# One more group's up-projection as seven half-size products, in a kernel whose order is written out by hand

## The chip, the core and the metric

The kernel runs on one core of one Trainium2 chip. The core has a matrix engine (TensorE, PE in the profile), a vector engine (VectorE, DVE), a scalar engine (ScalarE, ACT), GpSimd (POOL) and SyncE (SP), each with an instruction queue of its own, worked off strictly in order. The metric is the device time of one execution in microseconds (us); the time before is the median of 3 runs.

## The reference

Sliding-window attention with a distance bias feeds a two-layer network with a squared ReLU. Cut to what matters:

```python
# q, k, v: (8, 8, 576, 64); w_in: (512, 2048); w_out: (2048, 512), all float32
scores = (q @ k.transpose(0, 1, 3, 2)) / sqrt(64)
rel = pos[:, None] - pos[None, :]
scores = where((rel >= 0) & (rel < 128), scores - slopes * abs(rel), -1e9)
x = softmax(scores) @ v                    # -> 4608 tokens x 512
h = x @ w_in
g = maximum(h, 0) ** 2
out = g @ w_out                            # 4608 x 512, float32
```

## The kernel before

The 4608 tokens are cut into 9 groups of 512 (g = 0 to 8), and attention is cut into 40 blocks of up to 128 query tokens (m = 0 to 39), each of which sees its own keys and those of the block before. All matmuls are in bfloat16 with float32 sums in eight PSUM banks.

The program is a list of named tasks. `Plan.order()` does not choose an order: it reads the string `ORDER`, in which the tasks stand in the sequence in which they are emitted, each with its engine (`:a` ACT, `:d` DVE, `:g` POOL, `:s` SP, nothing for PE) and, where it needs one, the number of the PSUM bank, of the float32 buffer `f` (8 of them) or of the buffer `rt` (4). Each engine works its tasks off in that sequence; between engines semaphores keep the dependencies. An item is written `name:engine:places`.

The names, which all later sections use:

- `lkq<m>`, `lv<m>` load keys with queries, and values, from DRAM (POOL's queue, into rings of 4 and 9 tiles); `kqT<m>` turns a block of keys and queries with a DMA transpose (SP's queue, line 675, ring of 7).
- `s<m>.0/.1` are the scores of a block (PE, line 744: matmuls of 64 rows, two at a time on the two halves of the array, 8 per task or 12 for the blocks made of two 64-token ends: 10, 18, 28, 38); `e<m>.0` to `.3` the exponentials (ACT, line 776), `m<m>` the masks (DVE, line 771), `pv<m>` probabilities by values (PE, line 873; for the four two-end blocks lines 850 and 855), `r<m>`, `n<m>` the normalisation (DVE, lines 887 and 900), and `x<m>` the DMA transpose of the result into `xT` (SP, line 907).
- `u<g>.<half>.<e>` is the plain up-projection (line 1020): per task two blocks of 128 hidden units by 256 tokens, 8 matmuls of 256 columns. `relu...` (ACT, line 987) and `sq...` (ACT line 979 or DVE line 981) follow and write `g`.
- `f<g>.<u>.<p>` is the up-projection as seven half-size products (a scheme of Strassen's kind): hidden units and tokens are both halved, as are the 512 inputs, and for each of four column blocks u there are products p = 1, 2, 6, 5, 7, 3, 4, each of 4 matmuls of 256 columns (line 1115). `s1`, `s2`, `s5` copy partial sums from PSUM into an `f` buffer (line 429 on ACT, line 427 on DVE); `c11`, `c22`, `c12` add them with the ReLU in one DVE instruction (line 1136); product 4 takes the plain ReLU. `us<q>.<i>` are sums and differences of blocks of `w_in`, formed once (line 1061), and `ut<g>.<i>` differences of blocks of the group's `xT` (line 1084).
- `p<g>.<p>.<z>` is the down-projection, in all groups as seven half-size products (line 1270; two tasks of 8 matmuls each per product), with `S1` to `S4` (DVE, line 1416), `ws` (line 1228), copies `s1_<g>` and so on, combinations `c11_<g>` and so on (lines 1340, 1351, 1356), and stores `st<g>.<p>.<row>` (SP).

Groups 0, 1 and 2 have the plain up-projection, groups 3 to 8 that of seven products; the constant `G_UP` says from which group on:

```python
def ups(g):
    if g >= G_UP:
        return [("up", g, u, p) for u in range(4) for p in (1, 2, 6, 5, 7, 3, 4)]
```

One of the `us` steps overwrites a quarter of `w_in` in place, so it waits for the up-projections that read the plain weights:

```python
tops = [x for gg in range(G_UP) for x in g_up[gg]]
```

`ut<g>.0` needs all 512 tokens of the group, and the first two products only the first 256:

```python
xs = [x for m in blocks(g * 512, g * 512 + 512) for x in t_x[m]]
xe = [x for m in blocks(g * 512, g * 512 + 256) for x in t_x[m]]
```

Group 2 holds the attention blocks 8, 9, 10 (with 11) and 12. In the list before, the order on PE is: group 1 up, group 0 down, then group 1 down mixed with group 2 up (`u2.0` when the first half of its tokens is there, `u2.1` later), then group 2 down mixed with group 3 up (`f3`), and so on.

Of the kernel before, what the change touches and what calls it, by code (L numbers as in the profile page):

```python
# [100 lines left out]
squ2.0.3:d pv13.0::4 m13.1:d us1.3:d pv13.1::2 r13.1:d r13.0:d n13.0:d n13.1:d p1.6.1 s2_1:d:6 reluu2.0.2:a:3
reluu2.0.5:a:2 reluu2.0.4:a:0 kqT14:s kqT15:s kqT16:s lv14:g lkq17:g lv15:g lv16:g lkq18:g x10:s x12:s s14.0::4,6
s14.1::5,3 s15.0::2,1 p1.3.0 p1.7.0 p1.3.1 e14.0:a e14.2:a e14.1:a e15.0:a e14.3:a e15.1:a s15.1::3,2 s16.0::1,6
s16.1::5,4 e16.0:a e16.2:a e15.3:a e15.2:a e16.1:a p1.7.1 m14.1:d squ2.0.6:d c12_1:d m14.0:d u2.0.0::7 pv14.0::2
pv14.1::5 u2.0.1::3 c22_1:d m15.0:d reluu2.0.0:a:1 e16.3:a m15.1:d r14.0:d squ2.0.2:a r14.1:d n14.0:d pv15.0::6
r15.0:d n14.1:d pv15.1::7 m16.1:d reluu2.0.1:a:3 m16.0:d squ2.0.0:a u2.1.4::2 u2.1.7::5 pv16.0::3 pv16.1::4 kqT17:s
reluu2.1.7:a:1 squ2.0.1:a squ2.0.5:d reluu2.1.4:a:2 squ2.1.7:a r16.0:d n16.0:d r16.1:d r15.1:d n16.1:d n15.0:d
squ2.0.4:d n15.1:d u2.1.5::1 u2.1.6::3 reluu2.1.6:a:1 squ2.1.4:d reluu2.1.5:a:0 squ2.1.6:a u2.1.2::6 u2.1.1::3
reluu2.1.1:a:1 u2.1.0::1 u2.1.3::3 reluu2.1.0:a:2 squ2.1.5:a squ2.1.1:d us2.2:d reluu2.1.2:a:1 squ2.1.2:d squ2.1.0:d
S1.2.0:d s17.1::1,7 s17.0::2,4 p1.4.0 p1.4.1 p2.2.0::6 p2.1.0::5 p2.2.1 e17.0:a reluu2.1.3:a:0 e17.1:a squ2.1.3:a  # L110
m17.0:d us0.2:d S1.2.1:d e17.2:a e17.3:a S2.2.0:d m17.1:d S2.2.1:d lkq20:g lv20:g lkq21:g lv17:g s3_1:a:7 pv17.0::0
r17.0:d us3.2:d n17.0:d st0.3.0:s st0.7.2:s kqT18:s st1.2.0:s st0.2.1:s st0.7.3:s st1.2.1:s st0.2.0:s st1.7.2:s x13:s
x14:s kqT20:s x16:s x15:s s18.0::7,1 s18.1::4,3 pv17.1::2 p2.1.1 p2.5.0::0 p2.5.1 S4.2.0:d S4.2.1:d S3.2.0:d S3.2.1:d
r17.1:d e18.0:a e18.2:a s1_2:a:0 e18.1:a e18.3:a n17.1:d p2.6.0 p2.6.1 lv18:g c11_2:d m18.1:d m18.0:d f3.1.2::6
f3.0.1::2 f3.0.2::3 pv18::1,4 s1.3.0:a:3 s2_2:a:1 us1.2:d ut3.0:d ut3.1:d r18.0:d c11.3.0:d:0 ut3.2:d n18.0:d ut3.3:d
r18.1:d n18.1:d st1.7.3:s st0.3.1:s st1.3.0:s st0.4.3:s kqT21:s f3.0.5::7 f3.0.6 s2.3.0:a:3 p2.7.0 sqc11.3.0:a
s5.3.0:a:2 f3.0.7 f3.1.1::1 f3.1.5::4 f3.0.3 s1.3.1:a:4 c22.3.0:d:0 sqc22.3.0:a c12.3.0:d:2 c11.3.1:d:0 f3.1.6 f3.0.4
reluf3.0.4:a:1 s2.3.1:a:4 p2.7.1 s5.3.1:a:3 sqc12.3.0:d s5_2:d:2 c22_2:d lkq22:g lv21:g lkq23:g lkq24:g lv22:g lv23:g
kqT22:s lkq25:g s20.1::2,6 s20.0::7,3 f3.1.7 c22.3.1:d:2 f3.1.3 e20.0:a e20.2:a e20.1:a e20.3:a c12.3.1:d:3 m20.0:d
f3.2.1::7 p2.3.0 f3.1.4 m20.1:d pv21.0::6 pv20.0::4 f3.2.2::3 pv21.1::2 r20.0:d r21.0:d n21.0:d r21.1:d n21.1:d  # L120
sqc22.3.1:a sqc12.3.1:a reluf3.1.4:a:2 s1.3.2:a:4 sqc11.3.1:a sqf3.0.4:a sqf3.1.4:a p2.4.0 pv20.1::1 p2.3.1 n20.0:d
r20.1:d c11.3.2:d:3 s22.0::4,2 s22.1::3,6 e22.0:a e22.2:a e22.1:a e22.3:a p2.4.1 f3.2.6 f3.3.1::3 f3.2.5::2 s2.3.2:a:4
n20.1:d S1.3.0:d c12_2:d sqc11.3.2:d m22.0:d S2.3.0:d s1.3.3:a:3 x17:s st0.4.2:s st1.3.1:s st2.2.0:s kqT23:s x18:s
s23.1::6,0 s23.0::4,1 e23.0:a e23.1:a e23.3:a e23.2:a f3.2.7 s5.3.2:d:6 kqT24:s x21:s x20:s kqT25:s m22.1:d
c22.3.2:d:3 f3.3.6 f3.2.3 c12.3.2:d:2 sqc12.3.2:d f3.3.2::4 f3.3.5::1 f3.2.4 pv22.0::2 s2.3.3:a:6 s5.3.3:a:4 f3.3.7
# [5 lines left out]
lkq28:g st2.2.1:s st1.4.2:s st2.3.1:s st2.3.0:s st1.4.3:s kqT27:s kqT26:s p3.6.0 p3.6.1 ut4.2:d S3.3.0:d m24.0:d
c11_3:d S3.3.1:d ut4.3:d f4.0.7 c22.4.0:d:0 f4.1.2::4 f4.1.1::3 f4.0.3 p3.5.0::6 s1.4.1:a:5 sqc11.4.0:d f4.0.4 m24.1:d
f4.1.5::0 f4.1.6 c12.4.0:d:3 c11.4.1:d:2 S4.3.0:d m25.0:d m25.1:d pv24.1::4 pv24.0::1 s5.4.1:a:5 p3.5.1 f4.1.3
pv25.1::2 sqc22.4.0:a reluf4.0.4:a:1 r24.0:d r24.1:d n24.0:d n24.1:d pv25.0::1 r25.1:d r25.0:d n25.0:d n25.1:d
sqc12.4.0:d s2_3:a:6 sqc11.4.1:a s2.4.1:a:7 p3.7.0 f4.1.7 c22.4.1:d:2 c12.4.1:d:3 s5_3:d:5 S4.3.1:d s26.0::2,1
s26.1::4,7 e26.0:a e26.3:a e26.2:a e26.1:a p3.7.1 lkq30:g lv26:g lv28:g lv27:g lkq31:g lkq32:g kqT28:s st2.4.2:s x22:s
x23:s kqT30:s x24:s x25:s f4.2.1::2 f4.1.4 f4.2.2::4 reluf4.1.4:a:0 p3.3.0 s27.0::3,1 s27.1::7,0 e27.0:a e27.2:a
e27.3:a c22_3:d sqc22.4.1:d s1.4.2:d:7 c11.4.2:d:2 sqc12.4.1:d sqf4.0.4:d p3.3.1 f4.2.5::4 f4.2.6 s5.4.2:a:7 e27.1:a
p3.4.0 f4.2.3 s28.1::1,0 s28.0::7,3 c12_3:d s2.4.2:a:1 m27.1:d S1.4.0:d m27.0:d m26.0:d S2.4.0:d e28.0:a f4.3.1::6
f4.2.7 s1.4.3:a:0 f4.3.2::7 c11.4.3:d:1 e28.3:a kqT31:s st2.4.3:s st2.7.2:s kqT32:s st3.3.1:s sqc11.4.3:a f4.3.6  # L140
# [1339 lines left out]
```

## Time and profile before

| | |
|---|---|
| median of 3 runs | 289.09 us (289.02 to 289.82) |
| the profiled execution | 289.45 us, of which 286.1 us span from the first to the last instruction |
| granted TensorE clock | 1.00 |
| busy share of the span | PE 97%, weight loads 84%, DVE 85%, ACT 70%, POOL 37% |
| DMA | 39.60 MB, mean 138 GB/s |

The profile is one execution, recorded by the hardware. Busy time is the sum of the times in which an engine had at least one instruction under way. Neighbouring instructions overlap in their first and last stages, so the mean duration of an instruction is longer than the distance to the next one behind it. A row of the chain of waits gives its start, its length and what ran; a row of the timeline the same with the engine and, in brackets, the idle time before it.

### The profile page before, as it was taken

What the parts mean: (1) busy time and instruction counts of PE and PEld (TensorE: products, weight loads), DVE (VectorE), ACT (ScalarE), POOL (GpSimd) and SP (SyncE); (2) the same over time, 40 slices, a digit from 0 to 9 for tenths busy, and PEclk for the clock granted to TensorE, in tenths of its full rate; (3) what the DMA queues carried; (4) which work ended last, traced back from release to release, by engine and by line L of the source; (5) the groups of instructions that cost most, each with busy time, mean ns of one, the idle gap of its engine ahead of it and who ended that gap; (6) DMA issues with size and microseconds to landing.
All of it is one profiled execution on the core that took longest, in us unless ns stands there. A gap on an engine that the chain in (4) does not pass through costs nothing.

```text
span 286.1 us, 8477 instructions
## 1 busy us (share of the span) xinstructions
PE 277.3 (97%) x3403; PEld 240.3 (84%) x3404; DVE 242.2 (85%) x557; ACT 201.3 (70%) x397; POOL 106.3 (37%) x132
## 2 busy tenths in 40 slices
...
GB/s 127 166 196 169 182 200 166 168 154 151 177 151 180 179 155 196 173 141 183 146 163 148 151 173 151 147 187 210 170 93 21 57 93 2 21 95 35 23 112 124
DMA packets 171238, 39.60 MB, mean 138 GB/s; under 512 B 156736, under 2 KB 171200, under 8 KB 171200
## 3 DMA queue, kind: packets, MB, share of 16 engines
...
q8 instruction: 26, 0.43, 0.6%
...
## 4 chain that ended last, share of the span: by engine, by line
PE 93%; DMA 2%; ACT 2%; POOL 1%; DVE 1%; issue 0%; POOLq 0%
PE o L1270 38%; PE h L1115 26%; PE h L1020 14%; PE s L744 6%; PE pv L873 5%; DMA kq<-in_k_dram 2%; POOL kq L609 1%; PE tp L689 1%; ACT P L822 1%; PE xp L920 1%; PE o L1372 1%; ACT rt L987 1%; PE pv L855 1%; ACT masks L474 0%; PE s L813 0%; PE pv L850 0%
## 5 line engine op out<-in xcount | busy, mean ns | idle before, releaser
L1270 PEld LDWEIGHTS <-g 128*128 128x128 bf16 x704 | 67.0, 98 | 8.7
L776 ACT ACTIVATE P<-s 128x512 bf16<-128x512 f32 x120 | 64.0, 609 | 9.9 <-PE s L744 9.7
L1270 PE MATMUL o<-w_out_sb,g 128*128 128x256 bf16 x432 | 53.3, 273 | 0.0
L987 ACT ACTIVATE rt<-h 128x512 bf16<-128x512 f32 (+1 forms) x73 | 42.4, 598 | 14.4 <-PE h L1115 8.5
L1136 DVE CUSTOM_DVE_ANT_0 rt<-h,f 128x512 bf16<-128x512 f32 x72 | 47.8, 682 | 5.0 <-PE h L1115 2.5
L429 ACT ACTIVATE f<-h 128x512 f32<-128x512 f32 x62 | 36.3, 604 | 22.3 <-PE h L1115 18.3
L979 ACT ACTIVATE g<-rt 128x512 bf16<-128x512 bf16 x73 | 45.3, 641 | 3.7 <-DVE rt L1136 3.3
L1020 PE MATMUL h<-xT,w_in_sb 128*128 128x128 bf16 (+1 forms) x512 | 46.3, 246 | 0.1
...
L1020 PEld LDWEIGHTS <-w_in_sb 128*128 128x128 bf16 x512 | 39.0, 98 | 4.1 <-DVE xT L427 0.3
L1115 PEld LDWEIGHTS <-w_in_sb 128*128 128x128 bf16 x384 | 36.5, 98 | 4.5
L1115 PE MATMUL h<-xT,w_in_sb 128*128 128x256 bf16 x288 | 39.1, 273 | 0.0
L771 DVE TENSOR_TENSOR P<-P,masks 128x1024 bf16<-128x1024 bf16 x48 | 32.1, 681 | 4.7 <-ACT P L776 3.9
L1270 PE MATMUL o<-wsum,sums 128*128 128x256 bf16 x288 | 34.9, 273 | 0.0
L1270 PE MATMUL o<-wsum,g 128*128 128x256 bf16 x272 | 34.1, 273 | 0.0
L981 DVE TENSOR_TENSOR g<-rt 128x512 bf16<-128x512 bf16 (+1 forms) x72 | 28.6, 412 | 4.6 <-ACT rt L987 4.2
L1270 PEld LDWEIGHTS <-sums 128*128 128x128 bf16 x288 | 27.6, 98 | 3.5
L1115 PEld LDWEIGHTS <-us 128*128 128x128 bf16 x288 | 27.3, 98 | 3.6
L900 DVE TENSOR_TENSOR x<-pv,rec 128x256 bf16<-128x256 f32 x72 | 28.5, 416 | 0.7
L620 POOL DMA_DIRECT2D vt<-in_v_dram x28 | 24.9, 897 | 9.6 <-DMA kq<-in_k_dram 3.9
L429 ACT ACTIVATE f<-o 128x512 f32<-128x512 f32 x26 | 15.5, 602 | 16.1 <-PE o L1270 15.2
L1115 PE MATMUL h<-ut,us 128*128 128x256 bf16 x192 | 26.5, 273 | 0.0
...
## 6 DMA issues: line engine op xcount, KB each, us to landing
...
w_out_sb<-in_moe_w_out_dram POOLq DMA_DIRECT2D x4, 512.0 KB, 11.8
...
```

Source lines behind the costliest of these rows:

```text
L429: nc.scalar.activation(o, i, AF.Copy)
L620: nc.gpsimd.dma_start(tile_of(s_v[m])[0:n, :, 0:D], source(v, m))
L771: nc.vector.tensor_tensor(flat(Pt[sP.idx], w), flat(Pt[sP.idx], w), flat(mk, w), op=ALU.mult)
L776: nc.scalar.activation(flat(Pt[sP.idx], slice(2 * i, 2 * i + 2)), sS[i].tile.rearrange("p (j t) -> p j t", j=2)[:, :, lo:hi], AF.Exp, bias ...
L900: nc.vector.tensor_tensor(o, heads(sv)[0:n, :, 0:D], sr.tile[0:n, :].unsqueeze(2).to_broadcast([n, 4, D]), op=ALU.mult)
L979: nc.scalar.activation(o, i, AF.Square, bias=0.0, scale=1.0)
L981: nc.vector.tensor_tensor(o, i, i, op=ALU.mult)
L987: nc.scalar.activation(rts[srt.idx][:, 0:n], slot.tile[:, 0:n], AF.Relu, bias=0.0, scale=1.0)
L1020: nc.tensor.matmul(slot.tile[:, f * w:(f + 1) * w], w_in_sb[:, cc, fc * 128:(fc + 1) * 128], xT[:, cc, lo % (XR * 128):lo % (XR * 128) + w ...
L1115: nc.tensor.matmul(slot.tile[:, j * 256:j * 256 + 256], a, b_, start=fresh and j == 0 and c == 0, stop=c == 1, skip_group_check=True)
L1136: nc.vector._custom_dve(TENSOR_ADD_SAT, out=rts[srt.idx], in0=slot.tile, in1=other(), s0=FMAX, s1=0.0)
L1270: nc.tensor.matmul(slot.tile[:, z * 256:z * 256 + 256], stationary(c), moving(c), start=fresh and z == 0 and c == 0, stop=c == F - 1, skip ...
```

## The change

`G_UP` becomes 2, so that group 2 is projected up by seven products as well: the 16 tasks `u2...` with their 16 relus and 16 squares leave, and 28 tasks `f2...`, four `ut2`, twelve copies, twelve combinations, four relus and 16 squares come. The string `ORDER` is new from shortly after its 250th item on: the group-1 down-projection (`p1`) stands ahead of `f2` but for its last task, `f2` stands by itself, and then `p2` begins and runs mixed with `f3`. The `us` steps are done before `f2`. In all later groups tasks, banks and engines are placed anew, with the same tasks as before.

```diff
-G_UP = 3
+G_UP = 2
...
-s1_1:a:3 e10.0:a e10.3:a e10.2:a S1.1.1:d S2.1.0:d S3.1.1:d S2.1.1:d c12_0:d S3.1.0:d S4.1.1:d us2.1:d p0.4.1
-p1.5.0::7 e10.1:a p1.6.0 s12.0::2,6 s12.1::3,1 lkq16:g x9:s p1.5.1 e12.0:a e12.1:a e12.2:a e12.3:a c11_1:d m10.1:d
-m10.0:d us2.3:d pv10::2,5 u2.0.7::6 m12.0:d r10.0:d s5_1:d:4 r10.1:d m12.1:d n10.0:d n10.1:d u2.0.6::1 pv12.0::3
...
+p0.6.1 ws0.3:d s5_0:a:1 s2_0:a:2 S4.0.0:d S1.1.0:d ws1.2:d S1.1.1:d us2.1:d c11_0:d S2.1.0:d S2.1.1:d us2.2:d p0.3.0
+s8.0::2,0 s8.1::6,7 p0.7.0 p0.3.1 p0.7.1 squ1.0.4:a e8.0:a e8.3:a e8.1:a s9.1::0,7 s9.0::4,2 m8.0:d p1.1.0::5 p1.1.1
+c22_0:d S3.1.1:d c12_0:d e9.0:a e9.2:a e8.2:a e9.3:a S3.1.0:d m8.1:d ws1.3:d kqT10:s lv9:g lv10:g lv12:g lkq15:g
+lv15:g lkq13:g lkq14:g lkq16:g lv13:g lv14:g s10.0::1,0 s10.1::6,4 st0.7.2:s kqT13:s kqT15:s e9.1:a m9.1:d e10.0:a
+e10.1:a e10.3:a e10.2:a p1.2.0::7 pv8.1::2 pv8.0::1 p0.4.0 r8.1:d r8.0:d n8.0:d s1_1:d:3 n8.1:d m10.1:d m10.0:d m9.0:d
+p0.4.1 s12.0::6,1 s12.1::2,4 p1.2.1 e12.0:a e12.1:a e12.3:a e12.2:a s3_0:a:4 kqT14:s kqT16:s c11_1:d pv10::6,0 r10.0:d
+pv9.1::1 pv9.0::4 m12.0:d r9.0:d n9.0:d p1.6.0 r9.1:d n9.1:d pv12.0::3 p1.6.1 p1.5.0::1 m12.1:d r10.1:d n10.0:d
+pv12.1::6 r12.0:d n10.1:d s2_1:a:5 s13.0::4,2 s13.1::0,7 p1.7.0 p1.5.1 e13.0:a e13.2:a e13.3:a e13.1:a n12.0:d
+S4.1.1:d us3.2:d us2.3:d r12.1:d n12.1:d m13.1:d S4.1.0:d m13.0:d s15.0::6,7 s14.0::0,4 s14.1::2,3 s5_1:a:6 e15.0:a
+e14.0:a e14.1:a e14.3:a e14.2:a e15.1:a p1.7.1 pv13.1::6 pv13.0::0 p1.3.0 p1.3.1 c22_1:d m14.0:d r13.1:d r13.0:d
+n13.0:d n13.1:d m14.1:d m15.0:d c12_1:d lkq17:g lkq18:g lv16:g x8:s st0.7.3:s x9:s x10:s x12:s st0.3.0:s kqT17:s
+st1.7.2:s st0.3.1:s s16.0::0,7 s15.1::2,3 s16.1::6,4 e16.0:a e16.1:a e16.3:a e15.3:a e15.2:a p1.4.0 m16.0:d pv15.0::0
+pv14.0::7 pv14.1::1 f2.0.1::4 f2.0.2::3 s1.2.0:a:1 ut2.0:d ut2.1:d r14.0:d c11.2.0:d:2 ut2.2:d m15.1:d n14.0:d r14.1:d
+f2.0.5::2 f2.0.6 s5.2.0:a:7 e16.2:a s2.2.0:a:1 p1.4.1 f2.0.3 pv15.1::6 f2.0.7 f2.1.1::7 f2.3.1::3 r15.0:d c12.2.0:d:3
+n14.1:d r15.1:d ut2.3:d c22.2.0:d:1 n15.0:d m16.1:d n15.1:d sqc22.2.0:d s17.0::1,2 s1.2.1:a:1 e17.0:a e17.1:a f2.1.6
+s2.2.1:a:7 f2.0.4 lv18:g lkq20:g lkq21:g lkq22:g lv17:g f2.1.2::1 s17.1::0,2 f2.1.5::6 e17.2:a reluf2.0.4:a:1
+c11.2.1:d:0 sqc11.2.1:d sqc12.2.0:d f2.1.7 s5.2.1:a:1 e17.3:a f2.3.2::1 pv16.0::4 r16.0:d c22.2.1:d:3 n16.0:d
+f2.2.1::0 f2.1.3 f2.2.2::2 f2.1.4 pv16.1::4 c12.2.1:d:0 sqf2.0.4:a s1.2.2:a:1 sqc11.2.0:a c11.2.2:d:1 s1.2.3:a:7
+f2.2.6 f2.2.5::6 r16.1:d n16.1:d c11.2.3:d:2 sqc22.2.1:d f2.3.6 s2.2.2:a:1 f2.2.7 s5.2.2:a:2 f2.3.5::1 f2.2.3
+s2.2.3:a:7 c22.2.2:d:3 sqc11.2.2:d sqc11.2.3:d f2.3.7 sqc12.2.1:a s5.2.3:a:2 c22.2.3:d:1 sqc22.2.2:a m17.1:d m17.0:d
+S1.2.0:d f2.2.4 p2.1.0::4 f2.3.4 reluf2.2.4:a:2 reluf2.1.4:a:3 sqf2.1.4:d sqf2.2.4:a reluf2.3.4:a:0 sqf2.3.4:a f2.3.3
...
```

More of the change, by code (lines that the diff above doesn't have):

```diff
@@ L101 @@
[L101 to L125, printed above, removed]
@@ L131 @@
[L131 to L140, printed above, removed]
@@ new lines @@
+st0.2.1:s st1.2.1:s kqT18:s x14:s x13:s x15:s kqT20:s x16:s kqT21:s kqT22:s s18.1::3,5 s18.0::6,1 e18.0:a e18.2:a
+e18.1:a e18.3:a p2.5.0::2 p2.5.1 p2.6.0 p2.6.1 f3.0.1::5 f3.1.1::1 f3.0.2::3 s1.3.0:a:2 s1.3.1:a:3 S3.2.0:d c11_2:d
+m18.1:d n17.1:d S3.2.1:d ut3.0:d ut3.1:d f3.0.5::7 s5.3.0:a:0 f3.0.6 s2.3.0:a:5 f3.1.6 f3.0.3 f3.1.5::0 c11.3.0:d:0
+m18.0:d ut3.2:d c12.3.0:d:2 ut3.3:d f3.0.7 c22.3.0:d:1 s2.3.1:a:2 s5.3.1:a:6 f3.1.7 s2_2:a:5 f3.1.3 s20.0::7,3
+c22.3.1:d:3 sqc11.3.0:a sqc12.3.0:d c12.3.1:d:0 S4.2.1:d sqc22.3.0:a S4.2.0:d sqc22.3.1:d e20.0:a e20.1:a p2.7.0
@@ new lines @@
+f3.0.4 f3.1.4 reluf3.0.4:a:2 pv18::3,0 s22.0::5,7 reluf3.1.4:a:1 s5_2:a:2 e22.0:a e22.1:a r18.0:d n18.0:d r18.1:d
+n18.1:d p2.7.1 s22.1::3,1 s20.1::5,6 f3.1.2::0 f3.2.1::7 sqc12.3.1:d e20.3:a e20.2:a c22_2:d sqf3.1.4:d m20.0:d lv20:g
+lv21:g lkq23:g lkq24:g lkq25:g lkq26:g lv22:g st1.4.3:s st1.4.2:s kqT23:s kqT24:s st0.4.2:s x17:s kqT25:s st2.2.0:s
+kqT26:s x18:s c11.3.1:d:1 p2.4.0 f3.3.1::5 p2.4.1 m20.1:d e22.3:a s1.3.2:a:6 e22.2:a m22.0:d pv20.0::3 pv21.0::0
+pv20.1::1 pv21.1::6 r20.0:d r21.0:d n20.0:d r20.1:d r21.1:d p2.3.0 n20.1:d n21.0:d n21.1:d f3.2.2::3 c11.3.2:d:0
@@ new lines @@
+s1.3.3:a:3 sqc11.3.1:a f3.2.6 f3.3.6 f3.2.5::6 f3.3.2::3 s2.3.2:a:0 s5.3.2:a:6 s2.3.3:a:7 sqc11.3.2:a x20:s x21:s
+st0.4.3:s st2.2.1:s p2.3.1 S1.3.0:d S2.3.0:d c11.3.3:d:1 sqc11.3.3:a s3_2:a:3 c12_2:d f3.2.7 f3.3.5::0 f3.3.7
+s23.0::2,3 s23.1::4,1 c22.3.2:d:0 m22.1:d sqc22.3.2:d S3.3.0:d f3.2.3 f3.2.4 s5.3.3:a:6 e23.0:a sqf3.0.4:a e23.1:a
+reluf3.2.4:a:2 e23.3:a p3.1.0::2 p3.1.1 c22.3.3:d:0 c12.3.2:d:1 sqf3.2.4:d sqc22.3.3:d e23.2:a m23.1:d f3.3.4 f3.3.3
+c12.3.3:d:0 sqc12.3.3:d reluf3.3.4:a:2 sqf3.3.4:a pv22.0::4 pv22.1::1 r22.0:d n22.0:d r22.1:d s24.0::5,6 s24.1::7,3
@@ new lines @@
+sqc11.4.0:a f4.0.7 f4.1.4 c12.4.0:d:2 c12.4.1:d:3 r23.1:d c22.4.0:d:0 n23.1:d s26.0::5,7 p3.3.0 e26.0:a sqc12.4.1:a
+e26.1:a sqc12.4.0:d pv25.0::5 r25.0:d n25.0:d f4.2.1::1 pv25.1::6 r25.1:d n25.1:d s1.4.2:a:6 sqc22.4.1:a s2_3:a:1
+reluf4.1.4:a:1 p3.3.1 pv24.0::5 pv24.1::6 f4.2.6 f4.0.4 f4.3.1::0 f4.2.2::7 S3.3.1:d r24.0:d n24.0:d r24.1:d n24.1:d
+st2.3.1:s st2.4.3:s st2.3.0:s st2.4.2:s st2.7.2:s kqT27:s x22:s kqT28:s s2.4.2:a:4 reluf4.0.4:a:2 sqc22.4.0:a c12_3:d
+c11.4.2:d:3 S1.4.0:d s1.4.3:d:6 S3.4.0:d s27.0::3,4 s26.1::6,5 p3.7.0 p3.7.1 f4.3.2::7 e26.2:a e26.3:a e27.0:a e27.1:a
@@ new lines @@
+c22_3:d S2.4.0:d m26.1:d c11.4.3:d:0 sqc11.4.3:d m26.0:d s28.0::3,5 s28.1::4,6 lv26:g lv27:g lkq32:g lkq30:g lkq31:g
+lv31:g lv30:g x23:s x25:s x24:s kqT30:s kqT32:s kqT31:s p3.4.0 f4.3.6 sqf4.0.4:d e28.0:a e28.3:a e28.2:a p3.4.1
+f4.2.5::7 f4.3.5::4 s2.4.3:a:3 f4.3.7 s27.1::6,3 e28.1:a sqc11.4.2:a m28.0:d m27.0:d s5.4.3:a:6 c22.4.3:d:3 s5.4.2:a:5
+pv26.0::5 f4.3.3 f4.2.7 r26.0:d n26.0:d sqf4.1.4:a c22.4.2:d:1 f4.2.3 s3_3:a:6 c12.4.3:d:2 e27.3:a p4.1.0::5 pv26.1::3
+sqc12.4.3:d e27.2:a f4.2.4 f4.3.4 pv27.0::4 reluf4.2.4:a:2 sqc22.4.2:a reluf4.3.4:a:0 sqc22.4.3:a m27.1:d m28.1:d
@@ new lines @@
+st2.7.3:s st3.7.3:s st3.4.2:s st3.7.2:s st3.2.0:s st3.3.0:s m30.1:d S4.4.1:d m30.0:d f5.0.4 s5.5.1:a:3 f5.1.3
+c12.5.1:d:2 e32.0:a reluf5.0.4:a:3 e32.2:a lv32:g lkq34:g lkq33:g lkq35:g lkq36:g lv33:g lv35:g lv34:g p4.5.0::3
+pv30.0::1 f5.2.1::4 pv30.1::6 kqT33:s kqT34:s x27:s kqT35:s x28:s x26:s e32.1:a r30.0:d n30.0:d r30.1:d n30.1:d
+sqc12.5.0:a sqc22.5.0:a p4.5.1 f5.3.1::1 x30:s st3.4.3:s f5.3.2::6 f5.3.5::2 s1.5.2:a:5 c22.5.1:d:1 f5.2.6 S4.4.0:d
+s5.5.3:d:3 s1.5.3:a:1 e32.3:a f5.1.4 f5.3.6 sqc22.5.1:d c11.5.3:d:0 sqc11.5.3:d sqf5.0.4:d s2_4:a:7 s2.5.3:a:0
```

146 lines of the change are left out of this document (67 added, 79 removed).

## The prediction

> **What bounds the kernel now.** I read the page first, then the table of stages, then the chain of waits. The page's first part names TensorE (PE), and the chain that ended last runs almost wholly through it:
>
> ```profile
> PE 277.3 (97%) x3403; PEld 240.3 (84%) x3404; DVE 242.2 (85%) x557; ACT 201.3 (70%) x397; POOL 106.3 (37%) x132
> PE 93%; DMA 2%; ACT 2%; POOL 1%; DVE 1%; issue 0%; POOLq 0%
> ```
>
> A busy matmul row can hide stalls, so I asked for stages and for the spacing of the matmuls. The columns after the window are PE, weight loads, VectorE (DVE), ScalarE (ACT), GpSimd, the granted clock, DMA:
>
> ```profile
> 46.00:281.00 235.00, 235.00 (x2773) 205.58 (x2771) 213.30 (x459) 166.92 (x318) 73.85 (x89) 1.00 1.31 132
> 133.00:162.60 29.60, 29.60 (x388) 25.63 (x386) 28.41 (x64) 23.20 (x45) 14.54 (x17) 1.00 1.91 158
> 86.00:102.00 16.00, 16.00 (x209) 13.93 (x208) 11.51 (x30) 14.24 (x29) 5.23 (x7) 1.00 1.76 176
> ```
>
> ```profile
> 53.68 5.24 PE o L1270 x48
> ...
> 87.61 0.78 PE s L744 x24
> 88.39 0.98 PE o L1270 x8
> 89.37 0.87 PE h L1020 x8
> ...
> 265.44 13.10 PE o L1270 x120
> ```
>
> The reader should see three things. From 46 to 281 us PE is never idle, at a granted clock of 1.00. The spacing confirms it: 13.10 us / 120 = 0.109 us for each 256-column matmul, and the up-projection of today (line 1020) has the same, 0.87 / 8. So PE's work is the time, and what leaves PE's list leaves the time, if nothing new makes PE wait. In the second window DVE is busy 28.41 of 29.60 us and PE still does not wait; in the third, where today's third group is projected up, DVE is busy only 11.51 of 16.00.
>
> **What the change removes and adds on PE.** Group 2's up-projection is 16 tasks of 8 matmuls, 128 in all, and becomes 28 tasks (`f2.u.p`) of 4, 112 in all. That is 16 x 0.109 = 1.75 us less.
>
> The new list also breaks up score tasks. The next chain, read more closely, shows what a run of them costs:
>
> ```profile
> 116.58 0.87 PE o L1270 x8
> 117.45 0.55 PE s L744 x16
> 118.01 1.42 PE h L1115 x12
> ...
> 125.01 1.31 PE h L1115 x12
> ...
> 129.60 0.24 PE pv L873 x8
> ```
>
> A pair of score tasks (16 matmuls) takes 0.55, and the 12 matmuls behind it take 1.42 where 1.31 is their price, so a pair costs 0.66. A run of three (the row at 87.61 above) takes 0.78 + (0.98 - 0.87) = 0.89. One more task in a run is thus 0.23, and entering and leaving a run 0.66 - 2 x 0.23 = 0.20. No run of one is in this trace; by these two it is 0.43, and I bound it between 0.23 (no edge) and 0.66 (a whole pair). The old list has 27 pairs and 2 triples, the new one 21 pairs, 4 triples and 6 singles (`s17.0`, `s17.1`, `s20.0`, `s22.0`, `s26.0`, `s27.1`): -6 x 0.66 + 2 x 0.89 + 6 x 0.43 = +0.40 us, between -0.8 and +1.8 by the bounds. I take 0.40, because both parts of it come from rows.
>
> [...]
>
> PE's list therefore shrinks by 1.75 - 0.40 = 1.35 us.
>
> **What it adds elsewhere.** Rows for the prices, groups first, then two stretches of DVE's timeline and one of ACT's:
>
> ```profile
> L1136 DVE CUSTOM_DVE_ANT_0 rt<-h,f 128x512 bf16<-128x512 f32 x72 | 47.8, 682 | 5.0 <-PE h L1115 2.5 <-ACT f L429 1.7 <-issue 0.2
> ```
>
> ```profile
> 138.19 0.68 DVE L771 TENSOR_TENSOR P<-P,masks 128x1024 bf16<-128x1024 bf16 x1
> 138.79 0.68 DVE L1340 TENSOR_TENSOR f<-o,f 128x512 f32<-128x512 f32 x1
> 139.39 0.68 DVE L1416 TENSOR_TENSOR g<-g 128x1024 bf16<-128x1024 bf16 x1
> ...
> 145.38 0.24 DVE L887 RECIPROCAL rec<-pv 128x4 f32<-128x4 f32 x2
> 145.59 0.75 DVE L900 TENSOR_TENSOR x<-pv,rec 128x256 bf16<-128x256 f32 x2
> ...
> 150.94 0.41 DVE L981 TENSOR_TENSOR g<-rt 128x512 bf16<-128x512 bf16 x1
> 151.27 0.68 DVE L427 COPY f<-h 128x512 f32<-128x512 f32 x1
> ```
>
> ```profile
> 74.47 2.06 ACT L776 ACTIVATE P<-s 128x512 bf16<-128x512 f32 x4 [0.39 <-PE s L744]
> ```
>
> Instructions overlap their neighbours: a DVE instruction of 0.68 is followed after 0.60, one of 0.41 after 0.33, a reciprocal after about 0.08, and four ACT instructions take 2.06, 0.48 apart. I price by these pitches. DVE gets 12 combinations (L1136 form) and 4 differences `ut2` and 2 more squares, and loses one `x` copy and 10 copies to `f` which the new list gives to ACT: 12 x 0.60 + 4 x 0.33 + 2 x 0.33 - 0.33 - 10 x 0.60 = +2.9 us. ACT gets 22 copies and one `x` copy and loses 12 relus and 2 squares: about 9 x 0.48 = +4 us, of which it has idle time enough. None of this is priced on the path if it fits beside PE, which must be shown where the new work lies, because there `f2` no longer has a down-projection between its steps.
>
> From `f2.0.1` to `p2.1.0`, PE has 26 `f` tasks (26 x 0.437), `p1.4.1` (0.87), three `pv` (0.25 each) and two single scores: 13.9 us. DVE, from `ut2.0` to the last square that `p2.1.0` needs, `sqc11.2.3`: 11 at 0.60 (9 combinations, 2 masks), 16 at 0.33 (4 `ut`, 6 `n`, 6 squares) and 6 `r`: 12.4 us. ACT: 18 at 0.48 and 3 squares at about 0.5: 10.2 us. So DVE is full to 89%, less than the 96% that the second window bore with PE dense. What remains is latency: three snapshots per column block go through two or three free `f` buffers (1, 7, later 2), and each must be read by DVE before ACT may refill it. Walking the 26 tasks through these hand-overs, each of ACT's 0.6 and DVE's 0.68, I find PE waiting at three or four places for 0.03 to 0.1 us. I put 0.2 us on the path, with 0 and 2 as bounds.
>
> **What it moves.** Group 1's down-projection (`p1`) now comes as one block before `f2`, so all of group 2's tokens are needed at once, and attention runs ahead: scores of 12 to 16 come 3 to 5 us earlier in PE's work, those of 17 by 9. SyncE (SP) issues the transposes, in one queue with the stores:
>
> ```profile
> 68.19 6.75 SPq L675 DMA_TRANSPOSE kqT<-kq  x4
> 78.31 3.51 SPq L907 DMA_TRANSPOSE xT<-x  x2
> ```
>
> ```profile
> xT<-x SPq DMA_TRANSPOSE x2, 5.4
> ```
>
> ```profile
> xT<-x SPq DMA_TRANSPOSE x4, 8.0
> ```
>
> The second fence is for 78 to 82 us (us from issue to landing), the third for 91 to 102. PE work from the first `p0` (the row at 53.68 above) to `f2.0.1`: 27 `p` tasks (23.6), five pairs and two triples of scores (5.1), eleven `pv` at 0.25 and `pv10` with 24 matmuls at 0.24 / 8 (3.4): 32.1, so `f2.0.1` starts near 85.8 and `f2.0.5`, which needs `ut2.0` and with it `x12`, near 86.7. In SP's new queue stand `st0.7.2`, four `kqT` (6.75 us), `x8`, `st0.7.3`, `x9`, `x10`, `x12`. `c22_0`, which `st0.7.2` stores, follows 12 `p` and a pair (64.9) and lasts 0.68; with some 0.4 between engines and 0.7 for the store the four start near 66.7 and end near 73.5. Three `x` (3.51 / 2 each) and a store later, `x12` can go out near 79.3. Its data are there by then: `pv12.1` comes after 21 `p`, four pairs, `pv10` and five `pv`, near 76.6, and DVE then has `n12.0`, `S4.1.1`, two `us`, `r12.1` and `n12.1`, 2.0 us of pitch and 0.4 between the engines. So `x12` lands near 84.7 at 5.4 us, and `ut2.0` must start by 86.1: the landing may take 6.8 us before PE waits. `kqT17` follows `x12`, is out by 82 as today and has 8 us until `s17.0`, which stands ten tasks (4.7 us) behind `f2.0.1`. The weight sums `us` leave no wait: those that overwrite `w_in` now follow group 1, done when `p0` starts.
>
> The end is unchanged: the last combination and its stores follow the last matmul in both lists.
>
> ```profile
> 280.31 1.76 PE o L1270 x16
> 282.07 0.02 issue
> 282.09 0.69 DVE f L1356
> ```
>
> **Sum.** The profiled execution took 289.45 us, 286.1 of them span. 289.45 - 1.35 + 0.2 = 288.3; it lies 0.36 above the median of the runs, 289.09, so the median becomes 287.9. A measurement of this kernel can tell about 0.3%, 0.87 us, from no change: faster means below 288.22, slower above 289.96.
>
> **Rivals.**
> *Hand-overs slip (0.25).* The `f2` chains have margins of 0.1 us or less where `f2.1.2`, `pv16.0` and `s17.1` take banks that ACT has just read. For it: no `f` stage of today runs without a down-projection beside it. Against: PE shows no wait in 235 us. If half of the 28 tasks wait 0.1 us more, 14 x 0.1 = 1.4, and the time is 289.1: no change.
> *Transposes late (0.14).* If `x12` lands late, DVE stands at `ut2.0`, with every normalisation behind it, and PE at `f2.0.5`. It decides from 6.8 us; each further us is a us. The rows above give 5.4 at that time today and 8.0 fifteen us later, and one transpose, `kqT18` at 85.3, took 9.7:
>
> ```profile
> kqT<-kq SPq DMA_TRANSPOSE x1, 9.7
> ```
>
> At 9.7 it is 287.7 + 2.9 = 290.6 with no other stall: slower.
> *DVE is the bound (0.09).* DVE at 85% would be the engine that sets the time, and its +2.9 us would be added: 289.09 + 2.9 = 292.0. Against it stands DVE's 11.51 of 16.00 us where the new work goes. [...]
> That the change does not do what it says can be left out: the list holds `f2` tasks and no `u2` task.
>
> **Numbers.** Dense, 0.52: 287.9, with its own range 287.3 to 288.2 (score edges free, or 0.5 us of stalls). Range: from 287.4 to 290.6, which leaves out DVE as the bound and still later transposes at the top, and free edges at the bottom. Faster 0.52, same 0.25, slower 0.23.
>
> **What would show it.** Right: L1115 has 784 matmuls, L1020 384, L1136 84 instructions; PE is busy in all of 46 to 280; span about 285. A single score run costs 0.43. Wrong: idle of PE between 84 and 102, released by `xT` or `ut` (late transposes), by ACT `f` or DVE `rt` (hand-overs); or PE waits all over the kernel, released by DVE (DVE as the bound); or PE gaps in later groups, for which the sum has no term.

## The result and the profile after

The changed kernel takes 293.22 us (median of 6 runs, 292.02 to 293.94) beside 289.77 us for the kernel before in the same comparison (289.02 to 291.79): a ratio of 1.0108, with a 95% interval of 1.0068 to 1.0148. It is slower, where 287.9 was forecast; the range ended at 290.6. Ratios here and below leave disturbed executions out while the medians hold them all, so the two can differ a little.

The profiled execution of the changed kernel took 292.46 us, 290.7 of them span (before: 289.45 and 286.1). Lines of the source are one higher than before: the up product is L1116, the down product L1271. From the page: the busy row, the chain that ended last, and the granted clock in 40 slices of 7.3 us:

```profile
PE 277.4 (95%) x3388; PEld 239.8 (82%) x3388; DVE 245.1 (84%) x564; ACT 206.5 (71%) x406; POOL 106.3 (37%) x132
PE 86%; DMA 5%; POOL 3%; ACT 1%; issue 1%; DVE 1%; POOLq 0%
PEclk9999999999998999999999999999999999999999
```

PE has 15 matmul records fewer and is busy as long as before, 277.4 us beside 277.3: what left PE's list came back as matmuls that took longer (eight of `p1` take 1.55 us from 91.72 on, where eight take 1.05 from 84.52 on). And DMA holds 5% of the chain instead of 2%. The table of PE's waits between 45 and 286 us has one row only (total, times, longest):

```profile
PE h L1116 <- DVE ut L1085: 3.6, 1, 3.6
```

The chain between 79 and 93 us shows what stands behind it:

```profile
80.72 6.46 DMA xT<-x
87.18 3.15 issue
90.33 0.44 DVE ut L1085
90.77 0.05 issue
90.81 1.07 PE h L1116 x8
```

DVE stands at `ut2.0` until 90.33, and PE at `f2.0.5`: its eight matmuls before start at 86.13 and would at 0.109 us each be followed at 87.00; the next one starts at 90.81, a gap of 3.81 us (the row's 3.6 counts from the modelled end of the matmul before). The chain follows the transpose `x10` and calls the rest "issue"; the one that came last is `x12`. It went out at 82.07 and its own row (us from issue to landing) puts its arrival at 82.07 + 8.2 = 90.3, where DVE starts:

```profile
xT<-x SPq DMA_TRANSPOSE x1, 8.2
```

The table of stages shows a second loss behind the gap. After the window stand its length, PE, weight loads, DVE, ACT, GpSimd, the granted clock, DMA:

```profile
90.00:92.00 2.00, 1.19 (x11) 0.97 (x12) 1.64 (x5) 0.54 (x2) 0.00 (x0) 1.00 1.14 120
92.00:93.00 1.00, 1.00 (x7) 0.72 (x6) 1.00 (x3) 1.00 (x3) 0.00 (x0) 0.55 1.39 259
93.00:94.00 1.00, 1.00 (x8) 0.67 (x6) 0.31 (x3) 0.03 (x1) 0.58 (x1) 0.50 1.38 275
94.00:95.00 1.00, 1.00 (x13) 0.80 (x12) 0.74 (x2) 0.00 (x0) 1.00 (x2) 0.50 1.73 229
95.00:96.00 1.00, 1.00 (x8) 0.82 (x7) 1.00 (x4) 0.01 (x1) 1.00 (x2) 0.75 1.38 265
```

PE is busy in each of these microseconds from 92 on, but at a granted clock of 0.50 to 0.75. From the first matmul of `f2.0.5` to that of `p2.1.0` the kernel takes 90.81 to 105.45, 14.64 us; a later run without the gap (experiment 5) takes 12.96 for the same tasks. The low clock costs the difference, 1.68 us.

The span grew by 4.6 us: the gap 3.81, the low clock 1.68, and a start that came 0.81 later in this execution (the first score of block 7, next fence), together 6.3; against them 1.7 saved. The later start is chance: over twelve profiled executions with the same list up to there it lies between 37.6 and 39.9.

```profile
37.79 0.23 PE L744 MATMUL s<-kqT,kqf 64*128 64x128 bf16 x2
```

```profile
38.60 0.23 PE L745 MATMUL s<-kqT,kqf 64*128 64x128 bf16 x2
```

(The first is the kernel before, the second the changed one.) So below I also count from this score to the end of the span: 286.1 - 37.8 = 248.3 us before, 290.7 - 38.6 = 252.1 after.

### The profile page after: what moved, and what is told of

Read it like the earlier page. It is cut to its first block, busy times and chain, and to the rows that moved or that the text cites. A ratio compares the mean times of both kernels' runs of the same rounds, so it can differ in the third digit from the quotient of the medians.

```text
span 290.7 us, 8478 instructions
## 1 busy us (share of the span) xinstructions
PE 277.4 (95%) x3388; PEld 239.8 (82%) x3388; DVE 245.1 (84%) x564; ACT 206.5 (71%) x406; POOL 106.3 (37%) x132
## 3 DMA queue, kind: packets, MB, share of 16 engines
q0 software_dynamic: 115184, 18.10, 90.9%
## 4 chain that ended last, share of the span: by engine, by line
PE 86%; DMA 5%; POOL 3%; ACT 1%; issue 1%; DVE 1%; POOLq 0%
PE o L1271 36%; PE h L1116 30%; PE h L1021 8%; PE s L745 5%; PE pv L874 4%; DMA w_in_sb<-in_moe_w_in_dram 3%; DMA xT<-x 2%; POOL kq L610 2%; POOL vf L621 1%; PE tp L690 1%; PE o L1373 1%; ACT rt L988 1%; PE pv L856 1%; POOL w_in_sb L543 0%; ACT P L777 0%
## 5 line engine op out<-in xcount | busy, mean ns | idle before, releaser
L1271 PEld LDWEIGHTS <-g 128*128 128x128 bf16 x704 | 67.0, 98 | 9.3
L430 ACT ACTIVATE f<-h 128x512 f32<-128x512 f32 x79 | 45.5, 600 | 27.1 <-PE h L1116 20.0
L1137 DVE CUSTOM_DVE_ANT_0 rt<-h,f 128x512 bf16<-128x512 f32 x84 | 56.4, 684 | 6.7 <-PE h L1116 4.4
L1271 PE MATMUL o<-w_out_sb,g 128*128 128x256 bf16 x432 | 53.4, 273 | 0.0
L1116 PEld LDWEIGHTS <-w_in_sb 128*128 128x128 bf16 x448 | 42.7, 98 | 5.4
L1116 PE MATMUL h<-xT,w_in_sb 128*128 128x256 bf16 x336 | 46.4, 275 | 0.0
L980 ACT ACTIVATE g<-rt 128x512 bf16<-128x512 bf16 x71 | 43.0, 629 | 4.6 <-DVE rt L1137 4.2
L988 ACT ACTIVATE rt<-h 128x512 bf16<-128x512 f32 (+1 forms) x61 | 34.9, 598 | 12.0 <-PE h L1116 7.5
L1116 PEld LDWEIGHTS <-us 128*128 128x128 bf16 x336 | 32.2, 98 | 8.2 <-DVE ut L1085 3.9
L1271 PE MATMUL o<-wsum,sums 128*128 128x256 bf16 x288 | 35.2, 273 | 0.0
L1271 PE MATMUL o<-wsum,g 128*128 128x256 bf16 x272 | 34.9, 275 | 0.0
L1116 PE MATMUL h<-ut,us 128*128 128x256 bf16 x224 | 30.4, 273 | 3.6 <-DVE ut L1085 3.6
L1021 PE MATMUL h<-xT,w_in_sb 128*128 128x128 bf16 (+1 forms) x384 | 30.9, 237 | 0.7 <-DMA w_in_sb<-in_moe_w_in_dram 0.6
L1271 PEld LDWEIGHTS <-sums 128*128 128x128 bf16 x288 | 27.7, 98 | 3.3
L1021 PEld LDWEIGHTS <-w_in_sb 128*128 128x128 bf16 x384 | 27.0, 98 | 3.2 <-DMA w_in_sb<-in_moe_w_in_dram 1.4
L430 ACT ACTIVATE f<-o 128x512 f32<-128x512 f32 x31 | 18.5, 596 | 10.4 <-PE o L1271 9.8
```

Of the source, the lines that this page charges most:

```text
L430: nc.scalar.activation(o, i, AF.Copy)
L980: nc.scalar.activation(o, i, AF.Square, bias=0.0, scale=1.0)
L988: nc.scalar.activation(rts[srt.idx][:, 0:n], slot.tile[:, 0:n], AF.Relu, bias=0.0, scale=1.0)
L1021: nc.tensor.matmul(slot.tile[:, f * w:(f + 1) * w], w_in_sb[:, cc, fc * 128:(fc + 1) * 128], xT[:, cc, lo % (XR * 128):lo % (XR * 128) + w ...
L1116: nc.tensor.matmul(slot.tile[:, j * 256:j * 256 + 256], a, b_, start=fresh and j == 0 and c == 0, stop=c == 1, skip_group_check=True)
L1137: nc.vector._custom_dve(TENSOR_ADD_SAT, out=rts[srt.idx], in0=slot.tile, in1=other(), s0=FMAX, s1=0.0)
```

## The experiments

**Theory A:** the new order uses up the tokens of group 2 sooner than the stream of kq loads, kq transposes and x transposes can bring them; without that wait the change gains what its smaller list is worth. **Rivals:** the order costs time for another reason; the low clock is hidden somewhere; SP's queue alone, and not the DMA engines, makes the transposes late; a wait removed only makes the next transfer the last one. Each expectation below letters theories of its own.

**1. Transposes earlier on SP.**

```diff
-st0.7.2 ... kqT14 kqT16 x8 st0.7.3 x9 x10 x12
+st0.7.2 st0.7.3 ... x8 kqT14 kqT16 x9 x10 x12
```

> Only SyncE's queue differs from the changed kernel: st0.7.3 goes directly behind st0.7.2, and x8 ahead of kqT14. Theory A (late transposes): x12 is issued about 2.3 us earlier (near 79.8 instead of 82.1), the one gap of PE, 3.8 us at f2.0.5, shrinks to between 0 and 1.6 us, and the time falls by at least the 2.3 us; if the gap becomes so short that the granted clock stays at 1.00, by 1.7 us more: 288.5 to 291. Theory B (DVE is the bound of the stage, and the transpose only happened to be last): PE waits elsewhere in f2 instead, and the time falls by less than 1 us: 292 to 293. Theory C (the clock alone): unchanged as long as any gap is left.

Measured: 290.62 us, ratio 1.0036 (1.0005 to 1.0067). The waits of PE:

```profile
PE pv L874 <- DMA vt<-in_v_dram: 1.9, 1, 1.9
PE h L1116 <- DVE ut L1085: 1.1, 1, 1.1
PE s L745 <- DMA kqT<-kq: 0.2, 1, 0.2
```

The wait at `ut` shrinks from 3.6 to 1.1, the clock stays at 1.00 between 76 and 118, and the time falls by about 2.6 us, as theory A said: two entries of SP's list make up most of the loss. The way there was not quite the expected one: `x12` goes out at 82.56 in an execution that began 1.3 us later, so only 0.8 earlier and not 2.3, and it lands in 6.4 us instead of 8.2. But a wait that the changed kernel did not have is there now: `pv17` for the load `v17`, 1.9 us, which had been covered by the delay.

**2. The wait covered with other work.**

```diff
-s1.2.0 ut2.0 ut2.1 ... f2.0.5 ... r14 n14 m15.1 ... pv15.1 ... f2.1.1
+s1.2.0 e16.2 r14 n14 m15.1 c11.2.0 f2.1.1 pv15.1 ut2.0 ut2.1 f2.0.5
```

(and edit 1)

> As the run with x8 and st0.7.3 moved, and in addition f2.1.1, pv15.1 (0.7 us of PE) and on DVE r14, n14, m15.1 and c11.2.0 stand ahead of ut2.0 and f2.0.5, so that less waits behind the transpose. Theory A: the gap at f2.0.5 is below 0.8 us, granted clock 1.00 throughout, time 287.5 to 289, that is at or under the kernel before. Theory B (DVE is the bound of the stage): no better than the run without these moves.

Measured: 291.36 us, ratio 1.0059 (1.0031 to 1.0087).

```profile
PE h L1116 <- DVE ut L1085: 1.6, 2, 1.1
PE s L745 <- DMA kqT<-kq: 1.4, 2, 0.9
PE pv L874 <- DVE P L772: 0.5, 1, 0.5
```

Not better than edit 1 alone, which theory B (DVE as the bound) foresaw too; but DVE itself sits idle for 1.57 us before `ut3`. The wait at `ut2.0` falls to 0.5, and others of its kind come up: 1.1 one group later, at `ut3`, and 1.4 at the scores. This is what the last rival says.

**3. PE kept busy in the gap.** 33 matmuls of 256 columns ahead of the product that waits (their result is overwritten), 33 x 0.109 = 3.6 us.

```diff
+if (g, u, p) == (G_UP, 0, 5):
+    for _ in range(33): matmul(slot.tile[:, 0:256], ident, w_out_sb[:, 0, 0:256], start=True, stop=True)
```

> The changed kernel with 33 matmuls of 256 columns (3.6 us) on a bank that f2.0.5 overwrites, placed ahead of f2.0.5: they do no part of the computation and keep PE busy in the gap. The transpose is as late as in the changed kernel. Theory: the gap costs twice, once by itself (3.8 us) and once by the granted clock of 0.5 in the 3.5 us behind it (1.7 us). Then f2.0.5 starts at the same time, the clock stays at 1.00, and the time falls by about 1.7 us, to about 291.2. Rival: the low clock hides behind DVE in that stretch, and the time stays at 292 to 293.

Measured: 293.13 us, ratio 1.0118 (1.0086 to 1.0149), no gain where 1.7 us were expected. The clock is 1.00 in each window from 90 to 96 us, and the same tasks take 12.96 us again; the waits show where that went:

```profile
PE pv L874 <- DMA vt<-in_v_dram: 1.3, 1, 1.3
PE h L1119 <- DVE ut L1085: 0.9, 1, 0.9
PE h L1119 <- ACT f L430: 0.5, 1, 0.5
```

PE reaches `pv17` sooner and waits there for its load. In the changed kernel the low clock is thus part of the delay that hides the next late transfers; what it costs by itself is the matter of experiments 10 and 11.

**4. The order alone.** `G_UP` back to 3 with the new list, the third group as 16 plain units in place of `f2`.

> One part of the change alone: the new order with p1 as a block ahead, but group 2 projected up plainly (16 tasks u2.0, u2.1 in the place of f2, the us steps that overwrite w_in behind them). PE's work is 1.75 us more than the changed kernel's. Theory A: u2.0 needs only x8 and x9, u2.1 with x10 and x12 comes 7 us later, so PE has no gap and the clock stays at 1.00: the kernel before plus 0.4 us for the split score runs, 289.0 to 290.2, faster than the changed kernel by about 3 us. Rival (the order, with p1 first and attention early, is what costs, whatever the products): as slow as the changed kernel or slower, 293 or more.

Measured: 294.88 us, ratio 1.0184 (1.0149 to 1.0218), far from theory A's 289 to 290.2 and, by its number, what the rival said (293 or more). Its waits were mostly for DVE (`PE h L1019 <- DVE x`), and whether transfers stood behind them had to be asked: experiments 8 and 12.

**5. Loads in long packets.** The stream made quicker, and nothing else: rows of 512 neighbouring floats instead of eight pieces of 64. The rows hold other values, so the output of this version, and of 6, 8, 10 and 11 with the same edit, is not the reference's; only its time is of use.

```diff
+if m >= 8:
+    flat = t[b].rearrange("h s d -> (h s d)").rearrange("(s h d) -> s h d", h=H, d=D)
+    return flat[kb * 128:kb * 128 + blk[kb]]
 return s.rearrange("h s d -> s h d")
```

> The changed kernel, but the loads of q, k and v of blocks 8 and on take 512 neighbouring floats for each row of a tile instead of eight pieces of 64: same tiles, bytes, instructions and order, other values (so the attention of these blocks is not the reference's). Theory A (the new order is limited between 60 and 115 us by the stream of loads, kq transposes and x transposes through busy DMA engines): the loads land sooner than 8 us, the transposes land sooner too, the 3.81 us gap ahead of the first ut product falls under 1 us, and the clock stays at 1.00 after it: 287.0 to 288.8 us, ratio to before 0.990 to 0.997. Theory B (the transposes are late because SP issues them in a row behind a late pv and its own queue, whatever the DMA engines do): the gap stays over 3 us and the time between 291.5 and 293.5.

Measured: 288.61 us, ratio 0.9954 (0.9922 to 0.9986). Landing times between 60 and 115 us, first those of the changed kernel, then with long packets:

```profile
kq<-in_k_dram POOLq DMA_DIRECT2D x9, 128.0 KB, 8.0
kqT<-kq SPq DMA_TRANSPOSE x9, 8.0
xT<-x SPq DMA_TRANSPOSE x8, 8.2
```

```profile
kq<-in_k_dram POOLq DMA_DIRECT2D x10, 128.0 KB, 5.6
kqT<-kq SPq DMA_TRANSPOSE x11, 5.3
xT<-x SPq DMA_TRANSPOSE x8, 6.9
```

The transposes were not edited, and they land 1.3 to 2.7 us sooner: so the packets of the loads are part of what holds them, and not SP's list alone. The table of PE's waits is empty, and PE is dense at full clock:

```profile
46.00:280.00 234.00, 234.00 (x2766) 205.16 (x2765) 215.93 (x467) 173.77 (x330) 56.33 (x89) 1.00 1.02 132
```

With the same instructions in the same order, the loss is gone. From the first score of block 7 to the end it takes 286.43 - 39.86 = 246.6 us, 5.5 less than the changed kernel, which is its gap and its low clock (3.81 + 1.68).

**6. The same edit in the kernel before.**

> The kernel before with the same edit of the loads. Theory A: its transposes had some 11 us of slack, so nothing waited for them, and the time stays between 288.5 and 289.9 us (ratio 0.996 to 1.001). Theory B: the same. If instead it falls by 2 us or more, the kernel before was limited by its loads as well, and the changed kernel loses for another reason.

Measured: 288.92 us, ratio 0.9962 (0.9938 to 0.9986). That is 1.1 us by the medians, but not in the part that the loads feed: from the first score of block 7 to the end it takes 287.03 - 38.75 = 248.3, as before. The kernel before does not wait for its loads after 45 us. With the supply out of the way the change is worth 248.3 - 246.6 = 1.7 us in one trace of each; the two medians differ by 0.3 only, with intervals that overlap, since executions differ by about 2 us in their first 38 us alone.

**7. Four transfers ahead**: edit 1, the load `v17` ahead of `v18` and the transpose `x13` behind `kqT17`.

> The changed kernel with four transfers ahead: the store of f0.7.3 behind that of f0.7.2, the transpose x8 ahead of kqT14, the load v17 ahead of v18 and of three kq loads, the transpose x13 behind kqT17. The run with the first two of these measured 1.0036 with gaps of 1.3 us at ut2.0 and 2.0 us at pv17. Theory A: the wait for v17 goes, the rest of the stream stays as late: 289.0 to 290.4 us, ratio 0.998 to 1.003. Rival (each wait removed only lets the next transfer come last): another wait of 1 to 2 us shows between 105 and 120 us, and the time stays at 290.2 to 291.5.

Measured: 290.84 us, ratio 1.0017 (0.9986 to 1.0048).

```profile
PE s L745 <- DMA kqT<-kq: 2.1, 3, 1.2
PE h L1116 <- DVE ut L1085: 0.7, 1, 0.7
```

The wait for `v17` goes and the scores wait for their kq transposes instead, 2.1 us where it was 0.2. The median is the rival's (290.2 to 291.5), the ratio inside theory A's: of the loss of 1.1% at most 0.5% is left, and it cannot be told from the kernel before. It is the best version with the original loads that I ran, and no gain.

**8. The order alone, with long packets.**

> The run with the new order and a plain third group (1.0184) with the same edit of the loads. Theory A: its 5 us over before were waits for transfers, and they go: 288.9 to 290.4 us, ratio 0.997 to 1.003, and the run with products and this edit stands 1.0 to 2.0 us under it, which is what the products are worth by the row of 16 matmuls at 0.109 us. Theory B: it stays over 293.

Measured: 294.95 us, ratio 1.0180 (1.0142 to 1.0218): theory A missed again, by more than 4 us, and the time is that of experiment 4.

```profile
PE h L1022 <- DVE x L902: 2.3, 2, 1.5
PE s L746 <- DMA kqT<-kq: 0.8, 1, 0.8
PE pv L875 <- DVE P L773: 0.6, 1, 0.6
```

So the supply was not what held this version. Its plain units take PSUM banks that the attention of blocks 14 and 15 still holds until DVE has normalised them. Those banks were my choice when I wrote the list, so neither run speaks on the order.

**9. A fifth tile for kq loads**, in the version of experiment 7.

```diff
-SIZE = {"kq": 4, "v": 9, "kqT": 7, "P": 3, "x": 6}
+SIZE = {"kq": 5, "v": 8, "kqT": 7, "P": 3, "x": 6}
```

> The run with four transfers ahead, with a fifth tile for the loads of k and q (the v tiles go from 9 to 8 to make room, so the loads v14 and v38 come later in the list, and the load kq17 moves ahead of v14). The wait that this takes away is that of a kq load for the transpose four blocks back. Theory A (the stream is held up by this ring as well as by its packets): the loads kq17 and on start several us sooner, the waits of the scores for kqT (2.1 us in three places) fall under 0.8 us, and the time to 288.5 to 290.3 us, ratio 0.995 to 1.001. Rival (the DMA engines are full whatever the ring does): loads start sooner and land as late, 290.2 to 291.5 us.

Measured: 291.20 us, ratio 1.0036 (1.0013 to 1.0060), as the rival said. On GpSimd's timeline the load of kq17 starts at 67.05, where the changed kernel has it wait for a transpose until 77.48:

First experiment 9, then the changed kernel:

```profile
67.05 0.87 POOL L616 DMA_DIRECT2D kq<-in_k_dram  x1 [2.09 <-DMA kqT<-kq]
```

```profile
77.48 0.88 POOL L616 DMA_DIRECT2D kq<-in_k_dram  x1 [7.83 <-DMA kqT<-kq]
```

But with one more load under way they take longer. The median landings, of the three kq loads that the changed kernel issues from 59.5 to 68 us and of the four of experiment 9 from 57 to 68, and then the wait of the scores in 9:

```profile
kq<-in_k_dram POOLq DMA_DIRECT2D x3, 128.0 KB, 5.3
```

```profile
kq<-in_k_dram POOLq DMA_DIRECT2D x4, 128.0 KB, 8.9
```

```profile
PE s L745 <- DMA kqT<-kq: 3.5, 2, 2.7
```

The loads start earlier and take 3.6 us longer by the medians, and nothing is gained.

**10 and 11. A late `x12` by itself.** In the version with long packets, which has time to spare, `x12` goes behind a transpose and three stores; in 11 also the 33 matmuls of experiment 3.

```diff
-x10 x12 st0.3.0 kqT17 st1.7.2 st0.3.1
+x10 st0.3.0 kqT17 st1.7.2 st0.3.1 x12
```

> The run with long packets (288.61 us, no wait on TensorE after 45 us), with the transpose x12 moved on SP behind the store of f0.3.0, kqT17 and two more stores, some 5 us later. What a late x12 costs by itself, where the rest of the stream has time to spare. Theory A (a gap costs its own length and then half the clock for some 3.5 us): a gap of 3.5 to 4.5 us ahead of the first ut product, the granted clock near 0.5 behind it, and 5 to 6.5 us more than the run without the move: 293.5 to 295 us. Rival (the low clock is hidden in the full kernel): only the gap, 292 to 293 us.

> The run with long packets and the late x12, with 33 extra matmuls of 256 columns ahead of the product that waits (3.6 us of work whose result is overwritten), so that TensorE isn't idle for most of the gap. Theory A: the clock stays at 1.00 and the time is 1.2 to 2.0 us under that of the late x12 alone. Rival: the same time within 0.5 us.

Measured: 295.51 us and a ratio of 1.0216 (1.0166 to 1.0265) for the late `x12`; 295.67 us and 1.0147 (1.0100 to 1.0195) with the matmuls. The late `x12` costs 6.9 us against experiment 5 by the medians, a little over theory A's 5 to 6.5. By the medians the matmuls save nothing, by the ratios 0.0069, some 2.0 us, though the outer ends of the intervals overlap; the traces show a saving too. From PE's timelines, the product that waits and the next one, first of 10, then of 11:

```profile
92.62 1.89 PE L1119 MATMUL h<-ut,us 128*128 128x256 bf16 x8 [5.60 <-DVE ut L1088]
94.30 1.82 PE L1274 MATMUL o<-wsum,g 128*128 128x256 bf16 x8
```

```profile
93.30 1.08 PE L1122 MATMUL h<-ut,us 128*128 128x256 bf16 x8 [2.36 <-DVE ut L1088]
94.21 1.04 PE L1277 MATMUL o<-wsum,g 128*128 128x256 bf16 x8
```

The same eight matmuls take 1.82 us behind a gap of 5.6 and 1.04 behind one of 2.4. Up to `p2.1.0` it is 14.55 against 13.00 us: the low clock costs 1.55 us. Against experiment 5 the whole stretch from the first score of block 7 to the end is longer by 254.0 - 246.6 = 7.4 us, the gap of 5.76 and this 1.55. A late `x12` costs its own length and the low clock, and nothing is given back where the rest of the stream has time.

**12. The order alone, mended**: plain units in banks that are free, `s3` of group 1 and the masks of block 17 earlier, the original loads.

> The order alone, mended: the new order with a plain third group, but with its units in PSUM banks that are free when they start (in the run of 1.0184 they waited for banks that the normalisation of the attention still held), the sum s3 of the first group and the masks of block 17 earlier. A plain unit of the first half of the group needs x8 and x9 only; x10 and x12 are needed some 8 us later. Theory A (the order does no harm as long as no product needs all four blocks of the group at once): no gap over 1 us between 84 and 100 us, and 289.0 to 291.0 us, ratio 0.998 to 1.005. Theory C (the order itself costs 4 to 5 us): over 293 us again.

Measured: 293.09 us, ratio 1.0100 (1.0066 to 1.0134). The median is just over theory C's 293 us, the cost, some 2.9 us, under its 4 to 5 and over theory A's range.

```profile
PE s L743 <- DVE x L899: 1.0, 1, 1.0
PE pv L872 <- DVE P L770: 0.5, 1, 0.5
PE h L1114 <- ACT f L428: 0.4, 1, 0.4
```

No gap over 1 us, and no wait for a transfer: here, too, `x12` goes out at 82.07 and lands at 88.8, but the first unit that needs it, `u2.1.0`, starts at 98.95 and has 10 us to spare. So the late transpose is harmless with plain units. The time is not back at the old level all the same: 291.2 - 39.9 = 251.3 us from the score on, 3.0 over before, of which 1.9 are the waits in the fence (for DVE and ACT, at places that I chose); the rest I did not take apart. Whether the order alone can run as fast as the old one stays open.

## Why the prediction was wrong

*The step that failed* is the estimate of when `x12` lands, in the part on what the change moves. I had it go out at 79.3, arrive in 5.4 us at 84.7, 1.4 us before PE needs it. It went out at 82.07 and took 8.2. Both halves were off by 2.8 us. SP's timeline shows the first:

```profile
68.55 8.20 SPq L676 DMA_TRANSPOSE kqT<-kq  x4
76.85 1.82 SPq L908 DMA_TRANSPOSE xT<-x  x1
78.72 0.57 SPq L1310 DMA_DIRECT2D out_dram<-f  x1
79.39 4.02 SPq L908 DMA_TRANSPOSE xT<-x  x3
```

I started the four kq transposes at 66.7, behind the store in front of them, and gave them 6.75 us, the row of the kernel before. They start at 68.55, because the first waits for its load, and take 8.20, because the second issue holds SP for 3.76 us. The rows for both: SP's waits between 60 and 90 us, and the first two transposes alone:

```profile
SPq L676 <- PE pv L856: 3.8, 1, 3.8
SPq L676 <- DMA kq<-in_q_dram: 1.7, 1, 1.7
```

```profile
68.55 5.17 SPq L676 DMA_TRANSPOSE kqT<-kq  x2
```

The first of these rows puts the 3.76 us down to `pv10` on PE. That cannot be the cause: in experiment 5 the same issue is over at 70.90, and `pv10` starts there at 74.19. With the original loads and the new order this issue takes 2.7 to 4.2 us in every trace, with long packets 1.35 and 1.39 (5, 11) or 3.09 and 3.12 (10, 8), so what holds it stays open.

I had asked of `x12` whether its data are there, but not of the kq transposes in front of it, and in one queue they decide: `x8`, ready at 71.5, stands behind them until 76.85. (In experiment 5 the same four start at 68.11, though that execution began 1.3 us later, and take 6.01.) 0.8 of the 2.8 is the later start of this execution. The second half, 5.4 us, was the landing of the old order at that time. The four traces with the new entries on SP and the original loads (changed kernel, 3, 4, 12) have 6.7 to 8.2 us. Experiments 5 and 9 show that fewer packets shorten landings (the kq transposes from 8.0 to 5.3 us) and one more load lengthens them (the kq loads from 5.3 to 8.9), but more traffic is not what sets the new order apart: the mean DMA share between 60 and 115 us is 1.84, against 1.83 before. A likely part, not tested by itself: `x9`, `x10` and `x12` go out some 1.3 us apart and land in 5.6, 6.5 and 8.2 us (in experiment 12 in 6.1, 6.4 and 6.7), each longer than the one ahead, while the two transposes behind the 5.4 went out 2.3 us apart.

*The rival "transposes late"* had the right mechanism, place and point of decision (6.8 us of landing, or an issue later by as much) and a chance of 0.14. Its price was short in the term for what follows a gap: "each further us is a us" leaves out the low clock, 1.68 us here and 1.55 by experiments 10 and 11. With the gaps of 3.81 and 5.76 us the granted clock fell to 0.5 here, with waits of 1.1 to 2.74 us (the longest in experiment 9) it stayed at 1.00; between these no run has a gap, so where it begins is not shown. I had priced gaps of at most 2.9 us, and those by their length alone.

*The other terms* can be read in experiment 5, where nothing waits. PE dense: as forecast. The hand-overs of `f2`: 0.2 us forecast, no wait found. DVE: +2.9 forecast; in 46 to 280 it is busy 215.93 us against 212.82 before, +3.1. The rival that makes DVE the bound falls, DVE being busier there than before and PE never idle. A run of one score task, not in the old trace, was taken at 0.43; from the chain of experiment 5, 0.33 and 0.54 - 0.44 behind it:

```profile
92.16 0.33 PE s L748 x8
92.49 0.54 PE h L1119 x4
```

That is 0.43, so the edges of a score run are as priced. The list as a whole is worth 1.7 us from the first score on, where I had 1.35 - 0.2 = 1.15; the 0.55 more was not isolated. The sum would have put the profiled execution at 288.3; it took 292.46. The gap and the low clock are 5.5 of that, the late start 0.8; the time outside the span is 1.6 shorter in this execution (1.76 against 3.35 us), and the remaining -0.55 is what the list brought beyond the forecast.

*Shown* by removing it: the wait for the transfers is the loss (1, 5), transfers land sooner with fewer packets (8.0 to 5.3 us, 5) and later with one more load under way (5.3 to 8.9 us, 9), the new products and not the late `x12` alone make it count (12), and the low clock is a cost of its own (1.55 us, 10 and 11). *Open*: how much of the later landing of `x12` comes from standing in a row of transposes, and what holds the second kq issue. *Only argued*: that a full replan of loads, transposes and stores around the new order would keep the 1.7 us.
